# Four weight low parts moved from GpSimd to VectorE, a norm and a count read placed earlier, and a gate's high and low weights in one operand

## The chip, the cores and the metric

The kernel runs on one core of one Trainium2 chip. The metric is the time of one execution on the device, in microseconds (us); lower is better. The kernel before took 745.57 us, the median of three runs (744.25 to 747.7). The engines are named as the profile names them: PE is TensorE (PEld its weight loads), DVE is VectorE, ACT is ScalarE, POOL is GpSimd, SP is SyncE, which here only issues transfers. A q behind a name (PEldq, DVEq) is that engine's sequencer.

## The reference

Three layers follow each other. The first is attention with hashed buckets over 8 heads of 768 tokens by 64. Its output, reshaped to 768 x 512, goes through a routed mixture of 8 experts with a capacity, and the result through a dense mixture of 8 experts, whose gate is normalised over rows and columns in turn:

```python
logits = x @ w_gate                      # routed: one expert for each token
expert_idx = np.argmax(logits, axis=1)
...
h = np.maximum(np.einsum('ecd,edf->ecf', disp, w1), 0.0)
y = np.einsum('ecf,efd->ecd', h, w2)
...
logits = x @ w_gate                      # dense: every token through every expert
P = np.exp(logits - logits.max())
for _ in range(8):
    P /= P.sum(1, keepdims=True) + 1e-09
    P /= P.sum(0, keepdims=True) + 1e-09
    P *= N / E
for e in range(E):
    out += P[:, e:e + 1] * (np.maximum(x @ w1[e], 0.0) @ w2[e])
```

All inputs and outputs are float32. Each expert has w1 of 512 x 1024 and w2 of 1024 x 512.

## The kernel before

Products are made to nearly float32 accuracy from parts of fewer bits: an operand is split into a high part and a low part (the rest), and a product is high·high + high·low + low·high, three matmuls. ScalarE makes the high part by a copy to a narrower type, another engine the low part by a subtraction.

The program has three stages, one behind the other. Attention ends at about 124 us of the profiled span. The **routed stage** runs to about 255 us and the **dense stage** from there to the end.

In the routed stage the weights come as 32 halves of 1 MB (four for each expert). `load_next` issues a load into one of nine raw buffers (`raw`). `conv_next` calls `split_w` (L348), which for each half makes two tiles `hl` of 128 x 2 x 2 x 512: the high part by ScalarE (L355), the low part as a closure `lo` (L357). The low part runs on VectorE, but where the number of the tile, `(2 * i + z) % 8`, is 1 and the half i lies between 4 and `POOL_END`, which is 21, GpSimd runs it: this is so for i = 8, 12, 16 and 20. A raw buffer can be loaded again when its low parts are done. An expert's tokens are transposed into `dT` (`stage_a`, split by L1226 on ScalarE and L1227 on VectorE), multiplied by w1 (`g1`, matmuls L1255, result copied by ScalarE to `hs`, L1262), transposed again (`tr`, L1284, split into `hT` by L1285 on ScalarE and L1286 on VectorE) and multiplied by w2 (`g2`, L1297). The tiles `mm` in PSUM that take L1255 and L1284 are five buffers in turn, so a matmul into one waits until ScalarE and VectorE have read what stood there. What stands behind what on an engine is set by the order of the code: a list `steps` of products, with transposes put between, and conversions behind each step.

Tokens over the first 128 of an expert are multiplied by a second pass `E` (tiles `yl`, transposes by the matrix `twin`, L1271, split by L1277 on ScalarE and L1278 on VectorE). At the end of the routed stage, in `ffn` (L1354), the routed outputs are gathered back into `x` by GpSimd (`gather`, L1339). `scaled(0)` and `scaled(1)` (L1344) scale its halves on VectorE: a maximum (L1348), four small operations, three products (L1352). `norm` (L1034) makes the scale `scl` of the first weights of the dense stage: matmuls L1037 of one column, then L1039 and L1040 on VectorE. The high parts of these first weights, `first`, are two conversions L1524 on ScalarE that need `scl`.

`overflow` (L1465) holds the work for tokens beyond the second pass. The count of such passes, `nov`, is read on every engine from the tile `nums` (L1487), and a branch (L1488) skips the body; with these inputs the body is skipped. `put_end` (L1449) then scales the last outputs.

The dense stage begins with `combine` (transposes L1590 of `x`, matmuls L1595 and L1602). `logits2` (L1637) makes the second gate's logits for each half of the tokens from the high and low weights `wh` and `wl` (8 columns each, made at L1161 and L1162): 12 matmuls L1642, for four row blocks three each. ScalarE copies the result of 8 rows to `lt`, and `sink_in` (L1660) transposes `lt` in six pieces (L1663). The eight rounds of row and column sums follow between the products of the first expert.

Of the kernel before, what the change touches and what calls it, by code (L numbers as in the profile page):

```python
# [8 lines left out]
F32 = mybir.dt.float32  # L9
# [38 lines left out]
POOL_END = 4 * 8 - 2 - NRAW - NRAWX  # L48
HI_DVE = ()
LO_POOL = (1,)  # L50
# [11 lines left out]
SPAD = 24  # L62
# [166 lines left out]
def kernel(ctx: ExitStack, tc: tile.TileContext, consts, q, k, v, proj, wg, w1, w2, wg2, w12, w22, out, cap, dbg=None):  # L229
# [25 lines left out]
    wh = cpool.tile([P, 4, E], F16, name="wh")  # L255
    wl = cpool.tile([P, 4, E], F16, name="wl")
# [91 lines left out]
    def split_w(ts, raw, i, late=None):  # L348
        for z, t in enumerate(ts):
            sl = slice(2 * z, 2 * z + 2)  # L350
            n = (2 * i + z) % 8
            if 4 <= i < POOL_END and n in HI_DVE:
                V.tensor_copy(t[:, 0], raw[:, sl, :])
            else:
                nc.scalar.activation(out=t[:, 0], in_=raw[:, sl, :], func=AF.Copy)  # L355
            eng = nc.gpsimd if 4 < i < POOL_END and n in LO_POOL else V
            lo = lambda eng=eng, sl=sl, t=t: eng.tensor_tensor(  # L357
                out=t[:, 1], in0=raw[:, sl, :], in1=f32(t)[:, 0], op=ALU.subtract
            )
            if late is None:  # L360
                lo()
            else:
                late.append(lo)
# [651 lines left out]
    twin = sm.tile([P, P], F32, name="twin")  # L1015
    sm.tile([P, SPAD], F32, name="spad")
# [32 lines left out]
    def dispatch(first, last):  # L1049
# [74 lines left out]
        for r in range(2):  # L1124
            nc.gpsimd.tensor_tensor(
                out=twin[:, r * OVR:r * OVR + OVR], in0=ident[:, 0:OVR], in1=ident[:, OVR:P], op=ALU.add
            )
        square(wgf.rearrange("p c e -> p (c e)"), acc16[:, E, 0, 0:1])
# [225 lines left out]
    def ffn():  # L1354
        with ExitStack() as st:
# [38 lines left out]
            for s in steps:  # L1394
# [31 lines left out]
                if (nm, e, half) == ("w2", L - 1, 1):  # L1426
                    gather(0)
                    gather(1)
                elif (nm, e, half) == ("w1", L, 1):
                    scaled(0)  # L1430
                    norm(mm_tile(), 0, 0, 4)
                    first = [cut(z, lambda z=z: raw_t[4 * NV][:, 2 * z:2 * z + 2, :]) for z in range(2)]
                    for hi, _ in first:
                        hi()
                for _ in range((done > 2) + (done in CATCH)):
                    if done < 4 * NV - 3:
                        conv_next()
# [9 lines left out]
            return ps, extra, first  # L1447
# [17 lines left out]
    def overflow():  # L1465
        with ExitStack() as st:
# [20 lines left out]
            nov = nc.values_load(novi[0:1, 0:1], min_val=0, max_val=NOV)  # L1487
# [46 lines left out]
    last = ffn()  # L1534
    rawx.close()
    overflow()
# [95 lines left out]
    lt = x.rearrange("p t d -> p (t d)")[0:E, 0:S]  # L1632
# [4 lines left out]
    def logits2(a):  # L1637
        ps = bank()
        n = 0
        for c in range(4):  # L1640
            for w, b in ((wh, 0), (wh, 1), (wl, 0)):
                nc.tensor.matmul(  # L1642
                    ps[0:E, 0:HW], lhsT=w[:, c, :], rhs=xpart(a, c, b), start=(n == 0), stop=(n == 11),
                )
                n += 1
        nc.scalar.activation(out=lt[:, a * HW:(a + 1) * HW], in_=ps[0:E, 0:HW], func=AF.Copy)
# [13 lines left out]
    def sink_in():  # L1660
        ps = bank()
        for t in range(NT):
            nc.tensor.transpose(ps[:, t * E:(t + 1) * E], lt[:, t * P:(t + 1) * P], ident[0:E, 0:E])  # L1663
        V.tensor_tensor(
            out=pm, in0=ps[:, 0:NT * E].rearrange("p (t e) -> p t e", e=E), in1=bt(q[:, 1]), op=ALU.mult
        )
        V.tensor_reduce(out=gm[:, 0:1], in_=pm.rearrange("p t e -> p (t e)"), axis=AX.X, op=ALU.max)
# [309 lines left out]
```

## Time and profile before

| | |
|---|---|
| median of three runs | 745.57 us |
| lowest and highest | 744.25 and 747.7 us |
| the profiled execution's own time | 746.9 us |
| its span, first to last instruction | 745.0 us |
| granted TensorE clock, mean | 0.998 of full speed |
| PE busy | 727.3 us, 98% |
| DVE busy | 555.8 us, 75% |
| ACT busy | 461.6 us, 62% |
| POOL busy | 112.6 us, 15% |
| HBM read and written | 75.80 and 10.36 MB |

The profiled execution is 1.3 us above the median of the runs, inside their spread. Busy shares are averages over three stages of different kinds, so the views to read are those of single stretches: busy time by stretch, and the instructions in order of time with the idle time ahead of each and what ended it. A time in the first column of such a row counts from the start of the span.

### The profile page before, as it was taken

The page shows a single profiled execution, that of the slowest core. Times are in us where ns is not written, and L with a number is a line of the kernel's source. Part 1 is how long each engine was busy: PE and PEld are TensorE (multiplying, and loading weights), DVE is VectorE, ACT ScalarE, POOL GpSimd, SP SyncE. Part 2 cuts the span into 40 slices and gives each one's busy share as a digit, 9 for nine tenths or more (in the row PEclk, how much of TensorE's full clock was granted, in tenths as well). Part 3 has the DMA queues.
Part 4 walks back from the last instruction along what each step waited for, and adds up shares of the span by engine and source line. Part 5 has one row for each costly group of instructions (what it writes and reads, how often), then busy time and mean ns, then how long its engine had stood idle before and what let it go on. Part 6 is the DMA issues. An engine that isn't in the chain of part 4 may idle for free.

```text
span 745.0 us, 12322 instructions
## 1 busy us (share of the span) xinstructions
PE 727.3 (98%) x4764; PEld 467.7 (63%) x4764; DVE 555.8 (75%) x978; ACT 461.6 (62%) x756; POOL 112.6 (15%) x121
## 2 busy tenths in 40 slices
PE   8999999998999899999999999999999999999998
PEld 7888989776888656546446545545545545645654
DVE  5988999799996666887685785785785875866842
ACT  3799897589788468464754654664574475365420
POOL 5577964322103000000000000000000000000000
PEclk9999999999999999999999999999999999999999
DMA  9556649899966433521230131041033030000002
GB/s 223 120 129 176 160 148 377 309 383 388 363 249 202 131 111 113 176 99 67 83 106 38 57 114 57 5 166 57 1 118 108 1 114 1 0 1 1 1 1 84
DMA packets 59720, 93.87 MB, mean 126 GB/s; under 512 B 17507, under 2 KB 18963, under 8 KB 59658
## 3 DMA queue, kind: packets, MB, share of 16 engines
q1 hardware_dynamic: 52490, 81.16, 33.4%
q10 hardware_dynamic: 5888, 7.69, 3.2%
q0 software_dynamic: 1280, 4.20, 1.6%
q8 instruction: 39, 0.64, 0.4%
q14 instruction: 23, 0.19, 0.1%
HBM read 75.80 MB, written 10.36 MB: 116 GB/s over the span
## 4 chain that ended last, share of the span: by engine, by line
PE 63%; DVE 2%; ACT 1%; issue 0%; DVEq 0%; ACTq 0%
PE b L1879 32%; PE b L1804 25%; PE b L1847 4%; DVE hl L1527 1%; DVE s L1712 1%; PE b L1642 1%; ACT junk L1029 0%; PE b L1590 0%; PE b L1602 0%; DVE x L1895 0%; PE b L1595 0%; PE b L1037 0%; ACT hl L1524 0%; PE b L1689 0%; DVE x L1897 0%
## 5 line engine op out<-in xcount | busy, mean ns | idle before, releaser
L1879 PE MATMUL b<-hl,hT 128*128 128x512 f16 (+1 forms) x1176 | 252.0, 375 | 0.0
L1879 PEld LDWEIGHTS <-hT 128*128 128x128 f16 x1176 | 114.3, 98 | 129.0
L1804 PE MATMUL b<-xo,hl 128*128 128x384 f16 x1176 | 192.7, 326 | 0.0
L1804 PEld LDWEIGHTS <-hl 128*128 128x128 f16 x1176 | 114.7, 98 | 77.0 <-issue 0.8
L1527 DVE SCALAR_TENSOR_TENSOR hl<-raw,scl,hl 128x1024 f16<-128x1024 f32 x57 | 72.2, 1280 | 44.3 <-ACT hl L1524 44.3
L1524 ACT ACTIVATE hl<-raw,scl 128x1024 f16<-128x1024 f32 x57 | 63.1, 1135 | 28.5 <-DVE scl L1040 28.5
L357 DVE TENSOR_TENSOR hl<-raw,hl 128x1024 fp32r<-128x1024 f32 x60 | 75.3, 1299 | 6.2 <-ACT hl L355 5.9
L1029 ACT ACTIVATE junk<-raw 128x1024 bf16<-128x1024 f32 x64 | 67.1, 1048 | 1.0
L355 ACT ACTIVATE hl<-raw 128x1024 fp32r<-128x1024 f32 x64 | 63.8, 1065 | 0.0
L1255 PE MATMUL mm<-hl,dT 128*128 128x512 f32 x208 | 54.0, 406 | 3.8 <-DVE hT L1286 2.5
L1897 DVE SCALAR_TENSOR_TENSOR x<-b,q,x 128x512 f32<-128x512 f32 (+1 forms) x43 | 31.5, 737 | 34.4 <-PE b L1879 34.1
L781 POOL TENSOR_TENSOR plo<-pf,phi 128x768 f16<-128x768 f32 x30 | 49.7, 1667 | 23.9 <-ACT phi L777 11.8
L1776 ACT ACTIVATE hT<-tc 128x384 f16<-128x384 f32 x28 | 14.6, 523 | 60.2 <-DVE tc L1773 60.2
L1777 DVE SCALAR_TENSOR_TENSOR hT<-tz,hT 128x384 f16<-128x384 f32 x44 | 24.1, 555 | 36.1 <-ACT hT L1776 35.8
L1297 PE MATMUL y<-hl,hT 128*128 128x512 f32 x192 | 49.5, 401 | 0.0
L716 DVE TENSOR_REDUCE mz<-mm 128x1 f32<-128x384 f32 x96 | 47.5, 547 | 2.4 <-PE mm L709 2.1
L1524 ACT ACTIVATE hl<-s,scl 128x1024 f16<-128x1024 f32 x28 | 31.4, 1144 | 28.5 <-DVE s L1712 21.5
L770 ACT ACTIVATE pf<-mm 128x384 f32<-128x384 f32 x96 | 41.7, 487 | 8.0 <-PE mm L763 6.0
L1255 PEld LDWEIGHTS mm<-hl,dT 128*128 128x128 f32 x208 | 38.5, 192 | 12.9 <-DVE hT L1286 2.9
L763 PE MATMUL mm<-q,k 128*128 128x384 f32 x192 | 45.0, 353 | 0.0
L1297 PEld LDWEIGHTS y<-hl,hT 128*128 128x128 f32 x192 | 34.8, 188 | 7.4 <-issue 0.5
L777 ACT ACTIVATE phi<-pf 128x768 f16<-128x768 f32 x46 | 38.5, 846 | 1.2
(299 smaller groups left out, 1005.6 us busy)
## 6 DMA issues: line engine op xcount, KB each, us to landing
raw<-in_moe_w_dram SPq DMA_DIRECT2D x48, 1024.0 KB, 6.2
raw<-in_moe_w_dram SPq DMA_DIRECT2D x40, 256.0 KB, 5.4
raw<-in_moe_w_dram ACTq DMA_DIRECT2D x6, 1024.0 KB, 5.1
xd<-zer SPq DMA_DIRECT2D x13, 256.0 KB, 4.3
yd<-zer SPq DMA_DIRECT2D x7, 256.0 KB, 3.2
xe<-xd SPq DMA_DIRECT2D x7, 256.0 KB
qkin<-in_q_dram SPq DMA_DIRECT2D x8, 192.0 KB, 6.9
vin<-in_v_dram SPq DMA_DIRECT2D x4, 384.0 KB
```

What stands on the lines that cost most here:

```text
L355: nc.scalar.activation(out=t[:, 0], in_=raw[:, sl, :], func=AF.Copy)
L357: lo = lambda eng=eng, sl=sl, t=t: eng.tensor_tensor(out=t[:, 1], in0=raw[:, sl, :], in1=f32(t)[:, 0], op=ALU.subtract)
L716: V.tensor_reduce(out=mz[h][:, a, t:t + 1], in_=b.ps[:, 0:HW], axis=AX.X, op=ALU.max)
L763: nc.tensor.matmul(ps[:, 0:HW], lhsT=kk[h][:, tok(t)], rhs=qq[h][:, half(a)], start=(i == 0), stop=(i == 1))
L781: eng.tensor_tensor(out=lo[h, t], in0=pf[h, t], in1=hi[h, t], op=ALU.subtract)
L1029: nc.scalar.activation(out=junk[:, 0:n], in_=src, func=AF.Square, accum_out=acc)
L1255: nc.tensor.matmul(ps, lhsT=dT[e][:, a, c * P:(c + 1) * P], rhs=w(b, c), start=(n == 0), stop=(n == 4 * len(kinds) - 1),)
L1297: nc.tensor.matmul(ps, lhsT=t[:, a, half, f * P:(f + 1) * P], rhs=w(b, f), start=(n == 0), stop=(n == 2 * m - 1))
L1524: nc.scalar.activation(out=slot[n][:, 0], in_=src() if src else total[n], func=AF.Copy, scale=sw)
L1527: V.scalar_tensor_tensor(out=slot[n][:, 1], in0=src() if src else total.pop(n), scalar=sw, in1=slot[n][:, 0], op0=ALU.mult, op1=ALU.subtract,)
L1804: nc.tensor.matmul(ps, lhsT=w[:, a, c, j * P:(j + 1) * P], rhs=xo[:, o, b, c, :], start=(n == 0 and not again), stop=(n == 5), skip_group_ ...
L1879: nc.tensor.matmul(ps, lhsT=hT[:, a, 2 * r + f, t * P:(t + 1) * P], rhs=w[:, b, f, cs], start=(r == 0 and n == 0), stop=(r == 3 and n == 5),)
```

## The change

Four edits are made together.

1. `split_w` no longer chooses engines: every low part is made by VectorE. The four that GpSimd made stand now in VectorE's queue behind their neighbours.
2. In `ffn`, `norm` stands ahead of `scaled(0)`, and the two conversions `first` move from the step of w1's second half (expert L) to the end of the next step, behind the second transposes of pass E.
3. `nov` is read at that same place, by all engines, and handed to `overflow`, which branches on it where it did before.
4. `wh` and `wl` become one tile `whl` of 16 columns, so that `logits2` multiplies by high and low weights at once, with the high and the low part of the tokens: 8 matmuls for each half in place of 12, and the product of the two low parts is added. The 16 rows of `lt` are turned and summed by a matmul with `two`, two unit matrices under each other, in place of the transposes; GpSimd makes `two` by one small addition.

```diff
-POOL_END = 4 * 8 - 2 - NRAW - NRAWX
-HI_DVE = ()
-LO_POOL = (1,)
...
-SPAD = 24
+SPAD = 16
...
-    wh = cpool.tile([P, 4, E], F16, name="wh")
-    wl = cpool.tile([P, 4, E], F16, name="wl")
+    whl = cpool.tile([P, 4, 2, E], F16, name="whl")
+    wh, wl = whl[:, :, 0, :], whl[:, :, 1, :]
...
     def split_w(ts, raw, i, late=None):
         for z, t in enumerate(ts):
             sl = slice(2 * z, 2 * z + 2)
-            n = (2 * i + z) % 8
-            if 4 <= i < POOL_END and n in HI_DVE:
-                V.tensor_copy(t[:, 0], raw[:, sl, :])
-            else:
-                nc.scalar.activation(out=t[:, 0], in_=raw[:, sl, :], func=AF.Copy)
-            eng = nc.gpsimd if 4 < i < POOL_END and n in LO_POOL else V
-            lo = lambda eng=eng, sl=sl, t=t: eng.tensor_tensor(
+            nc.scalar.activation(out=t[:, 0], in_=raw[:, sl, :], func=AF.Copy)
+            lo = lambda sl=sl, t=t: V.tensor_tensor(
                 out=t[:, 1], in0=raw[:, sl, :], in1=f32(t)[:, 0], op=ALU.subtract
             )
...
+    two = sm.tile([P, E], F32, name="two")
...
+        nc.gpsimd.tensor_tensor(out=two[0:2 * E], in0=ident[0:2 * E, 0:E], in1=ident[0:2 * E, E:2 * E], op=ALU.add)
...
                 elif (nm, e, half) == ("w1", L, 1):
+                    norm(mm_tile(), 0, 0, 4)
                     scaled(0)
-                    norm(mm_tile(), 0, 0, 4)
+                elif (nm, e, half) == ("w2", L, 0):
                     first = [cut(z, lambda z=z: raw_t[4 * NV][:, 2 * z:2 * z + 2, :]) for z in range(2)]
                     for hi, _ in first:
                         hi()
+                    nov = nc.values_load(novi[0:1, 0:1], min_val=0, max_val=NOV)
...
-            nov = nc.values_load(novi[0:1, 0:1], min_val=0, max_val=NOV)
             with tc.If(nov > 1):
...
-    lt = x.rearrange("p t d -> p (t d)")[0:E, 0:S]
+    lt = x.rearrange("p t d -> p (t d)")[0:2 * E, 0:S]
...
         for c in range(4):
-            for w, b in ((wh, 0), (wh, 1), (wl, 0)):
+            for b in range(2):
                 nc.tensor.matmul(
-                    ps[0:E, 0:HW], lhsT=w[:, c, :], rhs=xpart(a, c, b), start=(n == 0), stop=(n == 11),
+                    ps[0:2 * E, 0:HW], lhsT=whl[:, c].rearrange("p z e -> p (z e)"), rhs=xpart(a, c, b),
+                    start=(n == 0), stop=(n == 7),
                 )
...
         for t in range(NT):
-            nc.tensor.transpose(ps[:, t * E:(t + 1) * E], lt[:, t * P:(t + 1) * P], ident[0:E, 0:E])
+            nc.tensor.matmul(
+                ps[:, t * E:(t + 1) * E], lhsT=lt[:, t * P:(t + 1) * P], rhs=two[0:2 * E], start=True, stop=True
+            )
```

The order of instructions on two engines shows the first two edits. Rows of the changed kernel carry its own line numbers, six to eight lower: its L349 is L357 of before, L1221 is L1227, L1280 is L1286, L1145 is L1151.

VectorE in the middle of the routed stage (low parts L357 of weights `hl`; `dT` and `hT` split for TensorE; `six`, `hs`, `idxg` and `ej` small tables of the dispatch). Before:

```order
L357 TENSOR_TENSOR hl<-raw,hl 128x1024
L1286 TENSOR_TENSOR hT<-mm,hT 128x512
L1151 TENSOR_SCALAR six<-six 128x6
...
L1227 TENSOR_TENSOR dT<-y,dT 128x512
L357 TENSOR_TENSOR hl<-raw,hl 128x1024 x2
L1286 TENSOR_TENSOR hT<-mm,hT 128x512
L357 TENSOR_TENSOR hl<-raw,hl 128x1024
L1286 TENSOR_TENSOR hT<-mm,hT 128x512
```

In the changed kernel:

```order
L349 TENSOR_TENSOR hl<-raw,hl 128x1024 x2
L1280 TENSOR_TENSOR hT<-mm,hT 128x512
L1145 TENSOR_SCALAR six<-six 128x6
...
L1221 TENSOR_TENSOR dT<-y,dT 128x512
L349 TENSOR_TENSOR hl<-raw,hl 128x1024 x2
L1280 TENSOR_TENSOR hT<-mm,hT 128x512
L349 TENSOR_TENSOR hl<-raw,hl 128x1024 x2
L1280 TENSOR_TENSOR hT<-mm,hT 128x512
```

Two of the four moved low parts show here, the second of a pair each time, ahead of a split of `hT`. GpSimd's queue loses all four, and `twin` and the new `two` follow each other there.

ScalarE at the end of the routed stage (`hT` L1277 is pass E's, `hl` L1524 the dense stage's first weights, `ysb` the copy that closes pass E). Before:

```order
L1262 ACTIVATE hs<-mm 128x512
L1524 ACTIVATE hl<-raw,scl 128x1024 x2
L1277 ACTIVATE hT<-mm 128x4x64
L334 DMA raw<-in_moe_w_dram 128x4x512
L1309 ACTIVATE ysb<-yl 128x512
```

In the changed kernel:

```order
L1256 ACTIVATE hs<-mm 128x512
L1271 ACTIVATE hT<-mm 128x4x64
L1519 ACTIVATE hl<-raw,scl 128x1024 x2
L1430 TENSOR_LOAD nums
L331 DMA raw<-in_moe_w_dram 128x4x512
L1303 ACTIVATE ysb<-yl 128x512
```

Pass E's copy now stands ahead of the two conversions, and the read of the count ahead of the next load. On VectorE at this place the two operations on `scl` stand ahead of `scaled(0)` in place of behind it, and the read of the count behind L1278.

## Rows read from the trace of the kernel before

**Rows 1.** Busy time by stretch: stretch, length, busy us of PE PEld DVE ACT POOL, PEclk, DMA.

```profile
180.00:190.00 10.00, 6.50 (x26) 4.70 (x25) 10.00 (x9) 7.45 (x11) 2.39 (x1) 0.87 1.05 389
190.00:200.00 10.00, 10.00 (x51) 8.29 (x51) 9.86 (x11) 7.76 (x12) 3.15 (x2) 0.96 1.05 338
192.00:240.00 48.00, 48.00 (x242) 39.92 (x240) 39.76 (x40) 42.49 (x60) 9.71 (x10) 1.00 0.76 262
240.00:256.00 16.00, 12.98 (x67) 9.92 (x66) 10.22 (x28) 6.28 (x12) 0.95 (x1) 1.00 0.54 161
```

**Rows 2.** Waits of PE from 256 to 742 us: total us, times, longest us.

```profile
PE b L1037 <- ACT junk L1029: 0.7, 1, 0.7
```

**Rows 3.** Timeline of DVE and POOL, 157 to 187 us: start, us, instruction, [idle before <-releaser].

```profile
159.14 5.75 DVE L357 TENSOR_TENSOR hl<-raw,hl 128x1024 fp32r<-128x1024 f32 x4 [0.66 <-ACT hl L355]
...
165.41 2.35 DVE L357 TENSOR_TENSOR hl<-raw,hl 128x1024 fp32r<-128x1024 f32 x2
...
171.04 2.51 POOL L357 TENSOR_TENSOR hl<-raw,hl 128x1024 fp32r<-128x1024 f32 x1 [8.38 <-ACT hl L355]
...
171.47 0.69 DVE L1286 TENSOR_TENSOR hT<-mm,hT 128x512 fp32r<-128x512 f32 x1 [0.20 <-ACT hT L1285]
...
172.08 1.50 DVE L1151 TENSOR_SCALAR six<-six 128x6 f32<-128x6 f32 x1
...
174.49 0.17 DVE L1156 TENSOR_SCALAR idxg<-six 128x6 int32<-128x6 f32 x1
...
181.52 2.39 POOL L357 TENSOR_TENSOR hl<-raw,hl 128x1024 fp32r<-128x1024 f32 x1 [7.97 <-ACT hl L355]
181.58 4.55 DVE L357 TENSOR_TENSOR hl<-raw,hl 128x1024 fp32r<-128x1024 f32 x2
...
186.06 0.68 DVE L1286 TENSOR_TENSOR hT<-mm,hT 128x512 fp32r<-128x512 f32 x1
```

**Rows 4.** Timeline, what TensorE waits for and uses, 168 to 204 us.

```profile
168.82 0.24 ACT L1137 ACTIVATE cand<-cand 128x48 f32<-128x48 f32 x1 [3.31 <-DVE cand L1134]
...
174.36 0.66 PE L1284 MATMUL mm<-ident,hs 128*128 128x128 f32 x4 [0.75 <-ACT hs L1262]
...
181.72 2.56 PE L1255 MATMUL mm<-hl,dT 128*128 128x512 f32 x10 [0.99 <-DVE dT L1227]
...
186.79 2.51 PE L1255 MATMUL mm<-hl,dT 128*128 128x512 f32 x6 [2.51 <-DVE hT L1286]
...
194.32 0.68 DVE L1227 TENSOR_TENSOR dT<-y,dT 128x512 fp32r<-128x512 f32 x1
...
198.68 4.36 PE L1255 MATMUL mm<-hl,dT 128*128 128x512 f32 x18
```

**Rows 5.** Timeline of the routed stage's end, 241 to 250 us.

```profile
241.81 1.00 PE L1271 MATMUL mm<-twin,hs 128*128 128x64 f32 x8
...
243.19 1.27 DVE L1352 TENSOR_SCALAR x<-x,q 128x512 f32<-128x512 f32 x3
...
244.75 1.15 ACT L1524 ACTIVATE hl<-raw,scl 128x1024 f16<-128x1024 f32 x1 [3.73 <-DVE scl L1040]
...
246.85 0.36 ACT L1277 ACTIVATE hT<-mm 128x256 fp32r<-128x256 f32 x1
...
247.72 2.11 PE L1297 MATMUL yl<-hl,hT 128*128 128x512 f32 x8 [1.64 <-DVE hT L1278]
```

**Rows 6.** The read, the branch, the first matmuls after it: sequencer durations (ns), then timeline.

```profile
L1487 PEldq TENSOR_LOAD <-nums x1: 488/488/488, 250.5 to 250.5; - x1
...
L1488 PEldq COMPARE_BRANCH x1: 3392/3392/3392, 251.1 to 251.1; - x1
...
254.83 1.50 PE L1590 MATMUL b<-ident,x 128*128 128x128 f32 x12 [1.38 <-DVE ys L1046]
```

**Rows 7.** The chain that ended last, 261 to 284 us: start, us, what.

```profile
261.54 2.04 PE b L1642 x12
...
283.69 0.47 PE b L1663 x6
```

More of the change, by code (lines that the diff above doesn't have):

```diff
@@ L1445, in ffn @@
                     puts.pop()()
-            return ps, extra, first
+            return nov, (ps, extra, first)
     def put_end(ps, extra, first):
@@ L1463, in put_end, with overflow @@
         V.tensor_copy(sv[:, 1:2], inv)
-    def overflow():
+    def overflow(nov):
         with ExitStack() as st:
@@ L1532, in cut @@
         return [hi, lo]
-    last = ffn()
+    nov, last = ffn()
     rawx.close()
-    overflow()
+    overflow(nov)
     put_end(*last)
@@ L1640, in logits2 @@
         for c in range(4):
-            for w, b in ((wh, 0), (wh, 1), (wl, 0)):
+            for b in range(2):
                 nc.tensor.matmul(
-                    ps[0:E, 0:HW], lhsT=w[:, c, :], rhs=xpart(a, c, b), start=(n == 0), stop=(n == 11),
+                    ps[0:2 * E, 0:HW], lhsT=whl[:, c].rearrange("p z e -> p (z e)"), rhs=xpart(a, c, b),
+                    start=(n == 0), stop=(n == 7),
                 )
                 n += 1
-        nc.scalar.activation(out=lt[:, a * HW:(a + 1) * HW], in_=ps[0:E, 0:HW], func=AF.Copy)
+        nc.scalar.activation(out=lt[:, a * HW:(a + 1) * HW], in_=ps[0:2 * E, 0:HW], func=AF.Copy)
     def token_scale():
```

## The prediction

> **What bounds the kernel now.** I read first the busy times by stretch, then TensorE's waits, then the order of time at each place where TensorE stands. TensorE works through all 48.00 us from 192 to 240 and, with one wait of 0.7 us aside, from 256 to 742 [rows 1, 2]: nothing can be won there but by giving it fewer matmuls. It stands in two stretches that the change touches. From 180 to 200 us it is busy 6.50 of the first 10 us and its granted clock averages 0.87 and then 0.96, while VectorE is busy 10.00 and 9.86 of each 10: there VectorE is the bound. From 240 to 256 TensorE works 12.98 of 16 us [rows 1]. The sum below is for these two places and for the matmuls that go.
>
> **The low parts.** A pair of lows on VectorE alone takes 2.35 us, so one takes 1.18 [rows 3]. The timeline shows three places where VectorE is slower while GpSimd makes a low: L1151, a table operation of 128x6, takes 1.50 us beside the low that starts at 171.04, where the like L1156 takes 0.17, so 1.33 is lost; the pair at 181.58 takes 4.55 in place of 2.35 beside the low at 181.52, so 2.20 is lost; the four from 159.14 take 5.75 in place of 4.70, 1.05 lost [rows 3]. L1286, which reads PSUM, takes 0.69 beside a GpSimd low and 0.68 without: it is not held. So with GpSimd's lows gone, VectorE gains 4.58 us over three places, and three lows of 1.18 cost it 3.53.
>
> This weighs against a rule. The Trainium skill ("Perfetto Trace Analysis", section "Optimizing Scalar/DVE Operations") says that where VectorE is saturated it may make sense to give some of its work to ScalarE or even GpSimd; it adds that between those two it might not help. By the first half alone the routed stage would get slower; the time that it gives is worked out as a rival below, from rows.
>
> What TensorE gets of it, place by place. VectorE's queue leads its old times by 1.05 from 159 on; the first moved low (1.18) stands ahead of an L1286, of which 0.66 is an idle time that VectorE had at 159.14 and that I take as filled: lead 1.05 − (1.18 − 0.66) = 0.53. TensorE's wait of 0.75 at 174.36 is for an `hs` of ScalarE, whose run began at 168.82 after 3.31 us of waiting for VectorE [rows 4]; so it shrinks by 0.53, to 0.22. Then L1151 is no longer held (+1.33) and the second low is added, of which 0.20 falls into the idle time ahead of L1286 at 171.47 (−0.98): lead 0.88, and the wait of 0.99 at 181.72 becomes 0.99 + 0.53 − 0.88 = 0.64. Then the pair takes 2.35 (+2.20): lead 3.08, and the wait of 2.51 at 186.79 becomes 2.51 + 0.88 − 3.08 = 0.31. TensorE is then **3.08 us** early [rows 3, 4].
>
> **The clock.** Over 180 to 200 the granted clock loses (1 − 0.87)·10 + (1 − 0.96)·10 = 1.7 us [rows 1]. It fell from 2.4 to 1.2 GHz right behind the waits of 0.99 and 2.51: the six matmuls at 186.79 take 2.51 us, 0.42 each, where the 18 at 198.68 take 4.36, 0.24 each [rows 4]. Behind single waits of 1.64 and 1.38 it stays at 1.00 from 240 to 256 [rows 1, 5, 6]. With 0.64 and 0.31 left I take it that it does not fall: **1.7 us** more; the ends are 0 and 1.7. The routed stage's gain is then 4.8 us.
>
> **Does VectorE keep up?** Behind the L1286 at 186.06 one more low of 1.18 now stands ahead of the next; VectorE's lead falls to 1.9 while TensorE's is 4.8, so TensorE closes in by 2.9. The next thing that it takes from VectorE with long queueing ahead is the `dT` of L1227, which ends at 194.32 + 0.68 = 195.00 and is used by the third matmul of the group at 198.68, at 199.16: 4.2 us of slack, 1.3 of it left [rows 4]. Behind that VectorE works 39.76 of 48 us [rows 1] and catches up. I count 0 for this; it is the step with the least cover, and has a rival. One raw buffer comes free later: GpSimd's third low ends at 181.52 + 2.39 = 183.91, and as the second of the pair on VectorE, behind the L1286 that would now end near 183.7, it would end near 186, 2 us later; the queue of nine buffers covers that. `two` is one small operation on GpSimd, which works 9.71 of 48 us: 0.
>
> **Norm ahead.** At the end of the routed stage ScalarE stands 3.73 us for `scl`, then makes two conversions of 1.15, and only then the copy L1277 of the transposes that TensorE finished at 241.81 + 1.00 = 242.81; the copy ends at 247.21, L1278 behind it ends when TensorE starts again, at 247.72, after waiting 1.64 [rows 5]. With the order changed, the copy can end at about 243.2. L1278 then waits for VectorE, which has the three products of `scaled(0)` until 243.19 + 1.27 = 244.46, and now the two `scl` operations ahead of them, which took the time to 244.75, 0.29: end of `scaled(0)` 244.75, L1278 done by 0.51 later (247.72 − 247.21), 245.26. TensorE is ready at 247.72 − 1.64 = 246.08, so the wait goes: **1.64 us**. The bounds are 0 and 1.64. The conversions come later, behind the copy, but their tiles are needed only in the dense stage, past the first matmuls at 254.83 [rows 6]; 2.3 us of ScalarE hide there.
>
> **The read ahead of the branch.** TensorE's sequencer spends 488 ns on the read at 250.5 and 3392 ns in the branch from 251.1, and then TensorE starts after 1.38 us of standing [rows 6]. The matmuls queued ahead end at 254.83 − 1.38 = 253.45, inside the branch (it ends at 251.1 + 3.4 = 254.5), so the branch is what ends last. With the read not directly ahead of it the branch can start 0.5 earlier, if its length is its own; if it merely waits for the matmuls ahead, nothing is won. At the new place the read can itself stop TensorE's queue for 0.49. Bounds: −0.6 to +0.5; I take **−0.5**, since the branch still runs 1.0 us after the last matmul ahead of it.
>
> **The gate.** Of `logits2`'s 24 matmuls for both halves 8 go. A dozen takes 2.04, so 8 × 0.17 = **1.36 us** less [rows 7]. The wider operand (16 columns of weights for 8) I take as free: the 18 matmuls at 198.68, with 128 columns of weights and 512 moving, take 0.24 each, 0.18 for the 384 that move here, no more than the 0.17 with 8 [rows 4, 7]. `sink_in` turns `lt` by a matmul in float32 in place of six transposes of 0.47 in all [rows 7]. In this trace a float32 matmul with `twin` has two records for each in the code: L1271 shows 8 records for the four in it [rows 5]. So 12 records; at the transposes' 0.078 each they take 0.94, **0.47 more**; at 1.00/8 = 0.125 each, 1.5, which is 1.0 more. I take 0.47, as the columns (8) are as few as in the transposes, and keep 1.0 for the range. The Trainium skill ("FP8 and Floating Point Precision", section "TensorE Precision Notes") has four passes for true float32, which would be 24 × 0.078, 1.4 us more and the total up by 0.9; the trace's two records speak for the half of it.
>
> **The sum.** 3.08 + 1.7 + 1.64 + 0.5 + 1.36 − 0.47 = 7.8 us less. The profiled execution's own time is 746.9, 1.3 over the median: 739.1 for such an execution, and from the median 745.57 − 7.8 = **737.8**.
>
> **The rivals.**
> - *The clock falls all the same.* The waits of 0.64 and 0.31 are still two within 6 us, and I have no row with such a pair. Then 1.7 stays lost: 739.5. Chance 0.15.
> - *TensorE runs into VectorE* between 186 and 206 us. VectorE is at 10.00 and 9.86 of 10 there [rows 1], and my cover is 1.3 us. If half of the routed gain is given back, 2.4: 740.2. Chance 0.10.
> - *The routed gain is not there at all* because another transfer or ScalarE (42.49 of 48 us busy, [rows 1]) comes last; only the other three edits count, 3.0: 742.5. Chance 0.06.
> - *Slower: VectorE is not held by GpSimd*, and its long operations are due to something else that stays. This decides at one point: whether the pair at 181.58 still takes some 4.5 us with GpSimd idle. Then VectorE, the bound from 180 to 200, has two lows more ahead of the L1286 at 186.06, 2.35 less 0.86 of idle time filled, +1.5; two more behind it, +2.3 where TensorE now has less slack than that; and one more stretch at the lower clock, +1.7. That is 5.5 less 3.0 of the other edits: 748. For it: VectorE is full. Against: three long operations of different kinds, all beside a GpSimd low, and short ones without. The skill's rule on offloading, above, gives this case. Chance 0.04.
> - My forecast has 0.65.
>
> **How the numbers follow.** The range takes in the first two rivals with the bounds of the read (+0.5 for −0.5), of the transposes (+0.5) and of the norm; downwards the read's −0.6 and an earlier start of the routed stage than I count, some 2 us: 735.0 to 741.8. About 0.5% (3.7 us) is what a measurement of this kernel can tell from no change: faster by over that is below 741.8, which holds the forecast and the first two rivals nearly whole, 0.88; the third and the upper edge of the second make 0.09 within it; slower 0.03.
>
> **What would show it.** Right: no low on VectorE over 1.3 us from 157 to 206; TensorE's waits ahead of its matmuls in 180 to 190 below 0.7 and the granted clock 1.00 in both stretches; no wait ahead of the second half of `yl`; a gap below 1 us ahead of the first transposes of the dense stage; 8 records for each half of the gate in 1.36 us; the six turns in about 0.9. Wrong: lows of over 2 us with GpSimd idle, a new wait of TensorE for `hT` or `dT` between 190 and 206, the granted clock below 1 after 180, a wait ahead of `yl` that names VectorE, or a branch that still ends 1.4 us behind TensorE's last matmul.

## The result, and the profile after

The changed kernel takes **738.89 us** (median of four, 738.52 to 739.36). Beside it the kernel before takes 746.63 (four, 744.25 to 748.32); the ratio is 0.9899, with an interval of 0.9868 to 0.993. That is 7.7 us less, faster by more than 0.5%. Forecast were 737.8 and a range of 735.0 to 741.8; the time lies 1.1 us over the forecast one because the kernel before, measured again beside it, is 1.1 us over the 745.57 that the forecast started from. The profiled execution after has a span of 737.2 us against 745.0.

The busy time by stretch answers to [rows 1]:

```profile
180.00:190.00 10.00, 9.49 (x45) 7.49 (x45) 9.86 (x13) 10.00 (x16) 0.00 (x0) 1.00 1.04 389
190.00:200.00 10.00, 10.00 (x52) 8.34 (x51) 10.00 (x12) 9.37 (x15) 0.60 (x1) 1.00 1.05 324
240.00:256.00 16.00, 15.15 (x88) 10.53 (x87) 12.60 (x30) 8.32 (x21) 0.00 (x0) 1.00 0.54 194
```

TensorE stands idle for 0.5 us from 180 to 200 in place of 3.5, its granted clock is 1.00 throughout, and VectorE is as full as before. VectorE's timeline, against [rows 3]:

```profile
160.00 4.62 DVE L349 TENSOR_TENSOR hl<-raw,hl 128x1024 fp32r<-128x1024 f32 x4
...
172.67 0.16 DVE L1145 TENSOR_SCALAR six<-six 128x6 f32<-128x6 f32 x1
...
180.83 2.35 DVE L349 TENSOR_TENSOR hl<-raw,hl 128x1024 fp32r<-128x1024 f32 x2
183.09 0.68 DVE L1280 TENSOR_TENSOR hT<-mm,hT 128x512 fp32r<-128x512 f32 x1
```

All three long places are gone: 4.62 for 5.75, 0.16 for 1.50, 2.35 for 4.55. The split of `hT` that began at 186.06 begins at 183.09. TensorE's timeline, against [rows 4]:

```profile
174.11 0.66 PE L1278 MATMUL mm<-ident,hs 128*128 128x128 f32 x4
...
180.96 3.93 PE L1249 MATMUL mm<-hl,dT 128*128 128x512 f32 x16 [0.51 <-DVE dT L1221]
...
193.54 4.38 PE L1249 MATMUL mm<-hl,dT 128*128 128x512 f32 x18
```

The first thing that does not fit the prediction stands here. The 10 and the 6 matmuls with 2.51 us between them [rows 4] are now 16 without a break, about 0.245 us each. The eleventh starts at 183.37 by its single record; but the split of `hT` that it waited for before ends only at 183.09 + 0.68 = 183.77. So this matmul no longer waits for that split at all. The experiments follow this up.

Where the time went is seen by the start of the same matmul in both profiles:

| matmul | before | after | lead | step |
|---|---|---|---|---|
| the transposes that need `xe` (L1233) | 144.17 | 144.65 | −0.48 | −0.48 |
| transposes of `hs` (L1284) | 174.36 | 174.11 | 0.25 | 0.73 |
| first with the new `dT` | 181.72 | 180.96 | 0.76 | 0.51 |
| the first of the six | 186.79 | 183.37 | 3.42 | 2.66 |
| the 18 of the next expert | 198.68 | 193.54 | 5.14 | 1.72 |
| second half of `yl` | 247.72 | 240.79 | 6.93 | 1.79 |
| first transposes behind the branch | 254.83 | 247.24 | 7.59 | 0.66 |
| behind the gate and its turns | 284.09 | 276.21 | 7.88 | 0.29 |

The end of the routed stage and the gate, against [rows 5 to 7], by three views of the kernel after (timeline; the branch's line, in ns; the chain that ended last):

```profile
238.96 3.81 PE L1291 MATMUL yl<-hl,hT 128*128 128x512 f32 x16
...
247.24 1.53 PE L1585 MATMUL b<-ident,x 128*128 128x128 f32 x12 [0.85 <-ACT junk L1022]
```

```profile
L1483 PEldq COMPARE_BRANCH  x1: 3337/3337/3337, 243.6 to 243.6; - x1
```

```profile
253.99 1.40 PE b L1637 x8
...
274.84 1.43 PE b L1659 x12
```

Both halves of `yl` run as one. The gap behind the branch is 0.85 for 1.38. Eight matmuls of the gate take 1.40 for 2.04, in both halves 1.28 less; but the turns take 1.43 for 0.47, 0.96 more.

### The profile page after: what moved, and what is told of

It reads as the page before. It is cut to its first block, busy times and chain, and to the rows that moved or that the text cites. A ratio compares the mean times of both kernels' runs of the same rounds, so it can differ in the third digit from the quotient of the medians.

```text
span 737.2 us, 12323 instructions
## 1 busy us (share of the span) xinstructions
PE 724.8 (98%) x4762; PEld 466.6 (63%) x4762; DVE 553.3 (75%) x982; ACT 461.3 (63%) x756; POOL 100.5 (14%) x118
## 4 chain that ended last, share of the span: by engine, by line
PE 85%; DMA 5%; DVE 4%; ACT 2%; issue 1%; SPq 1%; POOL 0%; ACTq 0%; DVEq 0%; POOLq 0%
PE b L1877 32%; PE b L1802 26%; PE b L1845 4%; PE mm L1249 4%; PE y L1291 4%; PE mm L755 4%; DMA raw<-in_moe_w_dram 3%; PE av L782 2%; PE mm L701 2%; PE mm L675 1%; DVE hl L349 1%; ACT hl L348 1%; DMA xd<-x,idxs 1%; DMA qkin<-in_k_dram 1%; PE mm L655 1%
## 5 line engine op out<-in xcount | busy, mean ns | idle before, releaser
L349 DVE TENSOR_TENSOR hl<-raw,hl 128x1024 fp32r<-128x1024 f32 x64 | 74.8, 1217 | 3.2 <-ACT hl L348 3.0
L1249 PE MATMUL mm<-hl,dT 128*128 128x512 f32 x208 | 52.4, 399 | 0.8 <-DVE dT L1221 0.8
```

The source lines that it names most:

```text
L349: lo = lambda sl=sl, t=t: V.tensor_tensor(out=t[:, 1], in0=raw[:, sl, :], in1=f32(t)[:, 0], op=ALU.subtract)
L1249: nc.tensor.matmul(ps, lhsT=dT[e][:, a, c * P:(c + 1) * P], rhs=w(b, c), start=(n == 0), stop=(n == 4 * len(kinds) - 1),)
```

## The experiments

Theory A was that GpSimd's reads hold VectorE (make its operations wait), that VectorE holds TensorE, and that the clock follows TensorE's waits. Leads below are differences of starts of the same matmul, as in the table, against the changed kernel unless another is named.

**The first edit alone**, on the kernel before (`eng = V` for every low part).

> The kernel before with the first edit alone: all low parts on VectorE. Theory A (GpSimd's lows hold VectorE's operations, and VectorE held TensorE and its clock): this edit alone gives the routed middle's whole gain, 5.6 us by the offsets of TensorE between the two profiles: 746.6 - 5.6 = 741.0. TensorE's waits at the three places are 0, about 0.5 and 0 us, the granted clock is 1.00 from 180 to 200 us, no low takes over 1.25 us on VectorE, and the end of the routed stage (second half of yl, the branch) looks as before. Theory B (the gain comes in part from the other edits, for instance from GpSimd's or ScalarE's queue): clearly less, 743 or more.

Measured: 742.78 us (five), ratio to before 0.9938 (0.9917 to 0.9959). Waits of TensorE in this run:

```profile
PE y L1228 <- DMA xe<-xd: 2.3, 1, 2.3
PE yl L1292 <- DVE hT L1273: 1.6, 1, 1.6
PE b L1585 <- DVE ys L1041: 1.4, 1, 1.4
```

The waits of the last two kinds are as before, as they should be. At the three places TensorE waits 0, 0.49 and 0 us, and no low takes over 1.23, as theory A has it. From 153 to 191 us (by the times of the kernel before) TensorE wins 5.86 us on the kernel before, though it enters that stretch 4.8 late: 1.9 us were lost before 127 us, the wait for the tokens' transfer `xe` is 1.3 longer than before (2.3), and behind it, at a clock of 0.90, 1.6 more are lost. By the trace the gain of this edit is A's. The time is less clear. The profiled execution is the slowest of the five (745.74), and the median is 1.8 over the 741.0; what the other four lost no trace shows. Against the kernel before, as measured beside it, the interval is 3.1 to 6.2 us less, which holds A's 5.6 and also smaller gains.

**GpSimd made to read**, and **GpSimd made only to write**, in the changed kernel:

```diff
+            if 4 < i < 21 and (2 * i + z) % 8 == 1:
+                for k in range(8):
+                    nc.gpsimd.tensor_tensor(
+                        out=twin.rearrange("p (c n) -> p c n", c=2), in0=raw[:, sl, 64 * k:64 * k + 64],
+                        in1=f32(t)[:, 0, :, 64 * k:64 * k + 64], op=ALU.subtract)
```

The second has in its place one subtraction of two columns and `for k in range(12): nc.gpsimd.memset(twin, float(k))`. Both then make `twin` anew.

> The changed kernel, with GpSimd made to read again what it read for its four lows, when it read it, in eight pieces of 128x128 each whose results nobody uses; VectorE still makes all the lows. Theory A (an operation on GpSimd that reads SBUF holds VectorE's operations): VectorE's rows beside the pieces grow again by 1 to 2 us at each of the three places, TensorE waits 2.5 us or more for the second hT, the clock falls, and since VectorE now has all lows to make too, the time is 744 to 746. If the hold ends with each small piece, VectorE loses less, some 0.3 us a piece: 740 to 742. Theory B (the long rows on VectorE had another cause than GpSimd's work, such as the order of its queue): 738.9, within 0.5.

> The changed kernel, with GpSimd kept busy at the same four places by a dozen fills of 128x128 that read nothing (behind a subtraction of two columns, which sets their start). Theory A1 (only GpSimd operations that read SBUF hold VectorE): VectorE's lows stay at 1.18 each and the time is 738.9, within 0.5. Theory A2 (any GpSimd operation on SBUF holds VectorE): rows as long as with the reads, TensorE waiting for hT and dT, 741 or more.

Measured: 745.2 us (ten, 743.81 to 749.17) and 739.39 (four, 738.26 to 741.23). VectorE and GpSimd with the reads:

```profile
184.30 2.81 DVE L349 TENSOR_TENSOR hl<-raw,hl 128x1024 fp32r<-128x1024 f32 x2
...
187.64 2.82 DVE L349 TENSOR_TENSOR hl<-raw,hl 128x1024 fp32r<-128x1024 f32 x2
```

```profile
183.48 7.85 POOL L354 TENSOR_TENSOR twin<-raw,hl 128x128 f32<-128x128 f32 x8 [1.91 <-issue]
```

and with the fills:

```profile
179.90 2.35 DVE L349 TENSOR_TENSOR hl<-raw,hl 128x1024 fp32r<-128x1024 f32 x2
...
182.77 2.35 DVE L349 TENSOR_TENSOR hl<-raw,hl 128x1024 fp32r<-128x1024 f32 x2
```

```profile
181.23 3.09 POOL L357 MEMSET twin<- 128x128 f32 x12
```

Beside reads a pair of lows takes 2.8 for 2.35, beside twelve fills 2.35, to the digit; in the run with fills the longer lows (1.31 to 1.35 for 1.21, by single records) all stand beside the two small adds, which read, that make `twin` anew. So it is GpSimd's reading that holds VectorE, not its being busy. The Trainium skill ("SBUF — State Buffer", section "SBUF: two separate sides") says of a VectorE operation with two SBUF inputs that it and a GpSimd operation that reads SBUF exclude each other for a whole instruction; these rows agree. In the kernel before, the pair from 181.58 ends at 186.13, which is 2.22 us behind the end of GpSimd's low at 183.91 [rows 3]: nearly the 2.35 that it takes alone, so until then next to nothing of it was done. The small pieces hold a low by 0.23 us, and they are held in turn: most of them take either 0.46 or about 1.32 us. Each pair loses less than it did, but the eight pieces last 7.85 us where one low took 2.4, so nearly every pair loses; the changed kernel's lead over this run grows by 4.9 us between 172 and 219. So the time fell within the expected 744 to 746 by another way than expected: no wait of TensorE behind 150 us is over 1.24 us, and the clock stays at 1.00. The table operation L1151, with one SBUF input, was held too [rows 3]; what else besides two inputs makes an operation liable was not tried.

A fourth held low, which the prediction did not count, stands in the kernel before beside GpSimd's last one, 2.82 us for 1.21:

```profile
196.85 2.67 POOL L357 TENSOR_TENSOR hl<-raw,hl 128x1024 fp32r<-128x1024 f32 x1 [12.93 <-DMA raw<-in_moe_w_dram]
...
197.79 2.82 DVE L357 TENSOR_TENSOR hl<-raw,hl 128x1024 fp32r<-128x1024 f32 x1
```

**Hold and tile apart.** Why did the eleventh matmul of the sixteen, the thirteenth of its group, stop waiting for `hT`? The program's own list of TensorE's instructions at this place, with the engine whose semaphore each waits for (Activation is ScalarE), before:

```
L1255 MATMUL mm<-hl,dT 128x512 x9
L1255 MATMUL mm<-hl,dT 128x512 [waits DVE_49]
L1255 MATMUL mm<-hl,dT 128x512 x5
```

and after:

```
L1249 MATMUL mm<-hl,dT 128x512 x9
L1249 MATMUL mm<-hl,dT 128x512 [waits Activation_49]
L1249 MATMUL mm<-hl,dT 128x512 [waits DVE_49]
L1249 MATMUL mm<-hl,dT 128x512 x4
```

Before, this matmul wrote into the PSUM tile that the split of `hT` on VectorE had yet to read; after, into one that only ScalarE reads, and has read by 182.54. The five tiles are not used strictly in turn, as the text above has it: which is taken is settled when the program is built, and it changes with the order of the code. Among variants of the code the place of one low part decides it here: with that of half 12 on GpSimd the matmul gets the tile of `hT`, otherwise the other. With (16,), (8, 12) or (12, 16) in this line, and the changed kernel, there are four kernels:

```diff
-            lo = lambda sl=sl, t=t: V.tensor_tensor(
+            eng = nc.gpsimd if i in (16,) and z == 1 else V
+            lo = lambda eng=eng, sl=sl, t=t: eng.tensor_tensor(
```

> The changed kernel with one low part, that of half 16 (the one beside the pair at 181.58 in the profile before), back on GpSimd. The program's list shows that the thirteenth matmul of the group from 180 us takes here, as in the changed kernel, the PSUM tile that the table product L1328 left, which ScalarE reads; in the kernel before it took the tile of the transposes that the split hT of VectorE reads. Theory E (the wait of 2.51 us came from that tile, and the hold alone costs little): VectorE's pair is held again, 4.5 in place of 2.35, but TensorE only waits some 0.7 us for the held low part, the clock stays at 1.00, and the time is 739 to 740. Theory F, that of the prediction (the hold of 2.20 us itself made the wait of 2.51): TensorE waits some 2 us for hT at 183 to 186, the clock falls, and the time is 742 or more.

> The changed kernel with the low parts of halves 8 and 12 back on GpSimd, those of 16 and 20 on VectorE. By the program's list the thirteenth matmul of the group from 180 us takes here the tile of the transposes that hT reads, as in the kernel before, while nothing on GpSimd holds the pair ahead of hT. Theory E (tile and hold together make the long wait): TensorE waits for hT, but only until the pair of 2.35 is done, some 0.3 to 0.8 us; the waits of 0.75 and 0.99 ahead of it come back; no fall of the clock or a short one: 740 to 741. Theory F (the hold alone): the same 0.3 us for hT, 740.5. Both say that VectorE's L1145 is held as L1151 was (about 1.5 us) and the four lows near 160 take 5.7. A wait of over 1.5 us for hT without a hold would say that the tile alone makes it.

> The changed kernel with the low parts of halves 12 and 16 back on GpSimd. By the program's list the thirteenth matmul of the group from 180 us takes the tile that hT reads whenever the low part of half 12 is on GpSimd, and the other one otherwise; so this run has tile and hold together, as the kernel before, where low16 had the hold alone and low8_12 the tile alone. Theory E (the two together make the long wait, and the wait the fall of the clock): TensorE waits 1.8 to 2.6 us for hT, the clock from 180 to 200 falls as before (0.87 to 0.96), and the time is 743 to 744.5. Theory F' (each costs its own small part, and they add): a wait of under 1 us, the clock at 1.00, 741 to 742.

| | tile read by ScalarE | tile read for `hT` |
|---|---|---|
| pair not held | changed kernel: 738.89 | low8_12: 740.83 (four) |
| pair held | low16: 740.52 (four) | low12_16: 745.13 (eight) |

In low16 the pair is held just as before:

```profile
181.53 4.57 DVE L350 TENSOR_TENSOR hl<-raw,hl 128x1024 fp32r<-128x1024 f32 x2
186.02 0.68 DVE L1281 TENSOR_TENSOR hT<-mm,hT 128x512 fp32r<-128x512 f32 x1
```

yet TensorE waits from 170 to 200 us only for `dT`; it falls a further 0.9 us behind the changed kernel up to 197, in steps of 0.13 to 0.40, and the clock stays at 1.00. (The median of 740.52 is above theory E's 739 to 740.) The waits of this stretch in low16, in low8_12 and in low12_16:

```profile
PE mm L1250 <- DVE dT L1222: 0.5, 1, 0.5
```

```profile
PE mm L1250 <- DVE dT L1222: 1.0, 1, 1.0
PE mm L1279 <- ACT hs L1257: 0.7, 1, 0.7
PE mm L1250 <- DVE hT L1281: 0.3, 1, 0.3
```

```profile
PE mm L1250 <- DVE hT L1281: 2.5, 1, 2.5
PE mm L1250 <- DVE dT L1222: 1.0, 1, 1.0
```

With the tile, and the pair not held, the wait for `hT` is 0.31 us, the figure of the prediction: the 2.51 of before less the hold of 2.20. With tile and hold it is 2.55, and the clock falls:

```profile
180.00:190.00 10.00, 6.49 (x27) 4.60 (x27) 10.00 (x9) 8.51 (x13) 2.40 (x1) 0.93 1.04 386
190.00:200.00 10.00, 10.00 (x50) 8.43 (x49) 9.86 (x13) 6.71 (x10) 0.00 (x0) 0.90 1.05 328
```

By the leads from 198 us on this is theory E: 0.9 us are lost with the hold of half 16 alone, 1.8 with the tile and the holds of 8 and 12, and 4.8 with the tile and the holds of 12 and 16, which is more than the sum of the two. F' falls, and F too: the hold of 2.20 alone does not make a wait of 2.51. The expected 743 to 744.5 for low12_16 was low by half a microsecond.

**The end of the routed stage**, its parts taken back one at a time. read_back reads the count in `overflow` again, right ahead of the branch; first_back makes the conversions in w1's step again; norm_back is

```diff
-                    norm(mm_tile(), 0, 0, 4)
                     scaled(0)
+                    norm(mm_tile(), 0, 0, 4)
```

> The changed kernel with the count read where it was, right ahead of the branch. Theory G (the branch takes TensorE's sequencer a length of its own, 3.34 to 3.39 us, and starts when the read ahead of it is done): the branch's record starts 0.45 to 0.5 us later against the last matmul ahead of it, and the gap ahead of L1585 is 1.35 to 1.4 in place of 0.85; 0.5 us slower. Rival H (the shorter gap came from what ScalarE and VectorE did in put_end): the gap stays 0.85.

> The changed kernel with the two conversions of the dense stage's first weights back in the step before, behind the norm that now stands ahead of scaled(0). Theory I (either half of the second edit frees ScalarE in time): scl is ready some 7 us earlier than before, the conversions end near the end of the transposes L1265, the copy L1271 is at most 0.5 us late and TensorE has no wait ahead of the second half of yl. Rival J (both halves are needed): a wait there of 1 us or more.

> The changed kernel with norm behind scaled(0) again and the two conversions still behind the second transposes of pass E. Theory I: the copy L1271 is free of the conversions, so TensorE has no wait ahead of the second half of yl; the conversions follow scl, some 2 us later than in the changed kernel, and are needed only in the dense stage. Rival J: a wait of 0.3 us or more there, or one behind the branch for the conversions or for the copy L1303 behind them.

The medians, 739.92 (two), 740.78 (two) and 740.7 (eight), are too near each other for effects of half a microsecond, so the profiles decide. TensorE's sequencer at the branch, in read_back and then in norm_back:

```profile
L1482 PEldq TENSOR_LOAD <-nums x1: 487/487/487, 245.5 to 245.5; - x1
...
L1483 PEldq COMPARE_BRANCH  x1: 3492/3492/3492, 246.1 to 246.1; - x1
```

```profile
L1483 PEldq COMPARE_BRANCH  x1: 3973/3973/3973, 244.3 to 244.3; - x1
```

Single records give the rest. With the read right ahead of it (the kernel before, lows_alone, read_back) the branch starts 1.82 to 1.93 us ahead of the start of the last matmul, with the read earlier (eleven profiles) 2.40 to 2.52 ahead: some 0.6 us earlier. From there it takes 3.33 to 3.97 us, and in all fourteen profiles TensorE starts 0.31 to 0.39 behind its end. Theory G holds for the start, and rival H falls. But the length is not the 3.34 to 3.39 that was expected: it differs by 0.6 us between profiles without any edit to the branch, so the gap is 0.85 to 1.48 with the early read and 1.38 to 1.59 with the late one. The two profiles of the changed kernel agree (3.34 and 3.33), so the length may belong to the program and not to the execution; what sets it was not tried.

In first_back and norm_back no wait ahead of the second half of `yl` is left: both halves run as one group of 16. ScalarE in each:

```profile
238.23 2.19 ACT L1519 ACTIVATE hl<-raw,scl 128x1024 f16<-128x1024 f32 x2
240.33 0.36 ACT L1271 ACTIVATE hT<-mm 128x256 fp32r<-128x256 f32 x1
```

```profile
238.47 0.39 ACT L1271 ACTIVATE hT<-mm 128x256 fp32r<-128x256 f32 x1 [1.40 <-PE mm L1265]
240.39 1.15 ACT L1519 ACTIVATE hl<-raw,scl 128x1024 f16<-128x1024 f32 x1 [1.54 <-DVE scl L1033]
```

With `norm` ahead the two conversions end soon enough that the copy starts only 0.4 us behind the end of its transposes; with the conversions moved the copy does not depend on when `scl` comes. Theory I: either half of this edit would have done.

**The turns**, six transposes of 16 rows and a sum on VectorE in place of the product with `two`:

```diff
-            nc.tensor.matmul(
-                ps[:, t * E:(t + 1) * E], lhsT=lt[:, t * P:(t + 1) * P], rhs=two[0:2 * E], start=True, stop=True
-            )
+            nc.tensor.transpose(ps[:, 2 * t * E:2 * (t + 1) * E], lt[:, t * P:(t + 1) * P], ident[0:2 * E, 0:2 * E])
+        V.tensor_reduce(
+            out=pm, in_=ps[:, 0:2 * NT * E].rearrange("p (t z e) -> p t e z", z=2, e=E), axis=AX.X, op=ALU.add
+        )
```

> The changed kernel, with the 16 rows of lt turned by six transposes (as before, but of 16 rows) and the two parts summed by one more VectorE operation, in place of the float32 product with two, which takes 12 records of 0.12 us, 1.43 in all. Theory C (a float32 product costs two records whose time is that of the weights' load, a transpose one of 0.08): the turns take 0.47 to 0.5 us, TensorE is 0.95 us earlier behind them, 737.9. Rival D (the added operation on VectorE delays the chain of rounds, for which TensorE then waits): no gain, 738.9, and a wait of TensorE at the maximum or at the first column sum.

Measured: 739.27 us (four, 735.98 to 741.4), where theory C expected 737.9. In the profiled execution TensorE comes to the branch 3.50 us later than in the changed kernel's, having waited 2.6 for `xe`, and leaves the turns 2.58 later: 0.92 won there, with no wait behind them. The six take 0.54 to their last end and 0.47 to the start of the next matmul, the added operation 0.25 on VectorE:

```profile
278.32 0.54 PE L1659 MATMUL b<-ident,x 16*128 16x16 f32 x6
```

```profile
280.34 0.25 DVE L1660 TENSOR_REDUCE pm<-b 128x48 f32<-128x96 f32 x1
```

Theory C, then, by the trace; the median does not show it.

**A version that combines** the turns with an earlier `dT`, beside the changed kernel once more:

```diff
-                mid = lambda acts=s[3:]: [act(a) for a in acts]
+                mid = lambda acts=s[3:]: [act(a) for a in acts] + [flush(len(los))]
...
-                        conv_next()
+                        conv_next(late=los if any(a[0] == "A" and 4 <= a[1] < E for a in steps[done][3:]) else None)
```

> The changed kernel once more, beside the kernels below. All theories: 738.5 to 740.5; TensorE waits ahead of L1227 near 144 us for the tokens' transfer, 1 to 2.6 us, which no edit touches, and where that wait is over 2.3 us the clock falls behind it (as in the runs with the low parts alone and with the six turns) and about 1.4 us more are lost: most of the spread of the times.

> The changed kernel with the six turns of 16 rows and one sum on VectorE in place of the product with two, and with the split of dT (L1221, from the fourth expert on) ahead of the pair of low parts that stood before it in VectorE's queue. If what is left of TensorE's waits in the routed middle, 0.3 and 0.5 us for dT, is that queue, both go, and with 0.95 us of the turns the time is 1.7 us less than the changed kernel's of the same call. Rival: the low parts, now 0.7 us later, are waited for instead, and only the 0.95 us are left.

Measured: 739.67 us (six, 738.79 to 741.93) and 738.46 (six, 737.32 to 742.89), spans of the profiled executions 737.9 and 736.6. Of the two waits for `dT`, 0.3 near 154 and 0.5 near 181, the second is gone whole. The first, 0.4, is left: there the edit leaves the order as it was, with a pair of lows still ahead of the `dT`. Both profiles have a new wait:

```profile
PE mm L1265 <- ACT hs L1256: 0.9, 1, 0.9
```

ScalarE stands 0.8 us ahead of that `hs` in the first and 2.1 in the second, for a releaser that the trace calls remote; the profile of the changed kernel that the sections above read has it not. What it is was not tried. By the table's kind of lead, the combined version wins 0.6 to this place, loses 0.3 to a longer branch, and wins 0.96 at the turns: 1.3 us, where 1.7 was expected. The medians, 1.2 apart, agree, but their ranges overlap: faster than the kernel before (ratio 0.9878, 0.9832 to 0.9923), and likely, but not shown, faster than the changed one.

## Why the prediction was right, and where not

The forecast difference, 7.8 us less, was met by the medians (7.7) and the spans (7.8). Term by term, by the table above:

| term | forecast | measured |
|---|---|---|
| TensorE's waits behind the lows | 3.08 | 3.90 |
| the clock | 1.7 | 1.72 |
| norm ahead | 1.64 | 1.79 |
| read ahead of the branch | 0.5 | 0.66 |
| fewer matmuls in the gate | 1.36 | 1.28 |
| the turns | −0.47 | −0.96 |
| entry into the stretch (`xe`) | 0 | −0.48 |
| sum | 7.8 | 7.9 |

- **The lows.** Held operations are GpSimd's doing, as the three rows were read (of the four lows from 159.14, though, only the first is held by a low, 2.08 us; the next two, 1.34 each, stand beside the two adds that make `twin`, which after the change run at 138). VectorE gains what was worked out: its `hT` at 186.06 comes 2.97 earlier (forecast 3.08), its `dT` at 194.32 comes 1.83 earlier, at 192.49 (forecast 1.9). TensorE's slack there, forecast 1.3, is 0.85 us: the `dT` ends at 193.17 and is used by the third matmul from 193.54, at 194.02. So VectorE keeps up, and that rival falls.
- **The step that failed** is "the wait of 2.51 at 186.79 becomes 2.51 + 0.88 − 3.08 = 0.31". It took for granted that the matmul waits for the same split after the change. That wait is gone whole, because the matmul has another PSUM tile; 0.31 is what it is where the tile stays (low8_12). In low16, where the matmul has the other tile, the wait is gone although the pair is still held. The first wait, too, went whole. The three steps are 0.73, 0.51 and 2.66, where 0.53, 0.35 and 2.20 were forecast; the last, the wait for `hT`, makes more than half of the 0.82 by which the term was too small.
- **The clock** came back as taken: behind 0.51 us it stays at 1.00, and also behind 0.7, 1.0 and 0.3 us within some 11 us (low8_12), so the rival of two small waits falls at this place. Behind 1.0 and 2.55 it falls (low12_16).
- **Norm ahead.** The wait of 1.64 went whole. The step is 0.15 more: in a run of matmuls each starts 0.23 us behind the one before, while a record lasts 0.39, and the wait is counted from the record's end. The text needed both halves of the edit; one does.
- **The read** was right in its mechanism, a branch that starts earlier once the read is not right ahead of it. The gap shrinks by 0.53 (1.38 to 0.85); the other 0.13 of the step is not the read's: most of it is the first matmul behind the wait ahead of `yl`, which took 0.33 us to the next start for 0.23 and went with that wait. That the branch's length differs by 0.6 us between profiles it could not know from one.
- **The turns** are the mis-sized term. Twelve records were right; 0.078 each was not, it is 0.119, near the upper bound of 0.125 taken from L1271. The argument that their few columns make them as quick as transposes fails: the weights' load of such a record takes 187 ns where that of a transpose of the same rows takes 137. The rule that was set aside, four passes for float32 (the Trainium skill, "FP8 and Floating Point Precision", section "TensorE Precision Notes"), gave 1.4 and was as near as the 0.47 taken. In the profile before, the two records of L1409 lie 0.43 us apart with 512 columns, where one of L1297 takes 0.23: that fits two passes for each record (an estimate from these two figures). So the count of records does not speak against the rule.
- **The slower rival** had its point of decision at the pair of 181.58, which takes 2.35 with GpSimd idle: it falls.

That the total came out within 0.1 us is in part luck: the waits and the branch gave more than forecast, and that paid for the dearer turns and for the late entry, which no term foresaw.

## What to carry to other kernels

Work given to an idle engine is not free if its reads hold the busy one: look for a long operation on the busy engine beside each operation of the other, and compare it with the same operation elsewhere. A wait in the trace names who came last for the buffer that the program happened to choose; when an edit moves instructions, compare the waits of the two programs' lists, not only their order, before a wait is carried over into the forecast. And compare starts of the same instruction in two profiles: half a microsecond shows there that medians two microseconds wide do not.

## What was not expected

The transfer `xe` near 144 us, which no edit touches, makes TensorE wait 0.4 to 2.6 us from one profile to the next. Up to 1.6 us the clock stays at 1.00 behind it (twelve profiles); at 2.3 and 2.6 us it falls, and TensorE loses 1.6 us more up to 158 us. The stretch from 140 to 150 us in lows_alone, in turn16 and in the changed kernel:

```profile
140.00:150.00 10.00, 7.74 (x35) 6.01 (x34) 4.38 (x6) 3.69 (x5) 0.49 (x2) 0.90 0.72 253
```

```profile
140.00:150.00 10.00, 7.36 (x30) 5.81 (x30) 3.75 (x4) 3.11 (x5) 0.00 (x0) 0.84 0.70 249
```

```profile
140.00:150.00 10.00, 8.71 (x42) 6.79 (x41) 5.46 (x6) 6.15 (x9) 0.00 (x0) 1.00 0.74 251
```

So this place alone differs by up to 3.9 us between two profiles, which is more than any edit here but the first gives. The start of the program differs too: against the kernel before, TensorE stands between 1.0 us ahead and 2.2 us behind at 127 us, and most of that is there by 20 us. In two profiles the clock falls there as well, to between 0.51 and 0.63 from 12 to 16 us, behind a wait of 2.59 us (read_back) and behind two of 1.49 and 1.25 us (low8_12), while behind 1.97 us it stays at 1.00 (low12_16). So what is said above of waits and the clock holds for the places named and is no general limit. A trace shows one execution of each kernel, so how much of the spread of the times these two places make is not shown.
